# Two passes of eight output rows in a long convolution's inverse transform, and a new order of the work

## The chip, the cores and the metric

The kernel runs on one core of a Trainium2 chip. The core has a matrix engine (TensorE, PE in the profile), a vector engine (VectorE, DVE), a scalar engine (ScalarE, ACT), a slower general engine (GpSimd, POOL), and SyncE (SP), which here only issues DMAs. The engines run their own instruction streams and wait for one another by semaphores. TensorE writes to PSUM, a memory of eight banks, and ACT or DVE must carry each result from there to SBUF (this is called an eviction below). The metric is the device time of one execution in microseconds.

## The reference

`x` is a 2048x448 array in bf16. The kernel computes a gated long convolution with a residual, and then an MLP that mixes along the sequence, with a residual:

```
qn  = layernorm(x)
ks  = sum over t of k_pad[:, t:t+S, :] * shift_k[:, 3-t]     # causal filter of four taps, per channel
kv  = ks * v
y   = irfft( rfft(kv, 2S) * rfft(ssm_k, 2S) )[:S] + kv * ssm_D # long convolution, per channel
h   = x + qn * y
g   = layernorm(layernorm(h))
u   = gelu( einsum("bsd,sf->bdf", g, w1) + b1 )              # 448 x 1792
out = h + ( einsum("bdf,fs->bds", u, w2) + b2 ).transpose    # 2048 x 448
```

## The kernel before

The sequence index is split as s = 16 q + r, with q on the 128 partitions and r (16 "rows" of 448 channels) along the free dimension. The transforms are two small matrix products with a shuffle between partitions in the middle.

The stages, by the names that the order lists use:

- `loads`, `kT`: the filter `ssm_k` arrives channel-major in four chunks of channels (128, 128, 128 and 64) and is transposed on TensorE (L1028). `dummy` products (L1015) stand at the start and between the chunks; they compute nothing that is used.
- `kv`: `k` is transposed (L956), and the four-tap filter is made of small TensorE products with diagonal matrices `DG` (built at L941). In each, two tiles of 64 array rows work side by side (L982). DVE multiplies the result by `v` on its way out of PSUM (L997).
- `k1`, `u1`: the first half of the transform, of the filter and of `kv` (L1049), four tiles of 32 columns side by side; evictions L1059; then a shuffle from SBUF to SBUF by DMAs of the POOL and SP queues (L1065) through a ring of four buffers.
- `k2`, `u2`: the second half (L1084), evicted in place (L728, L729, L731, L732) into `TK` and `TU`, 16 planes each.
- `i1`: DVE multiplies each plane of `TU` with one of `TK`, all four real products at once (L1150), into a ring of four buffers. TensorE applies the inverse of the second half (L1167) to a pair of planes at a time, all 16 output rows in one product of 64 array rows and 128 columns. An eviction (L728) puts the result back into `TU`, and DMAs (L1190, and L1179 for the last pair) shuffle it to `TZ`: for each plane 112 partitions by the POOL queue and 16 by SP.
- `i2`: for each output row r, two products (L1289) read all of `TZ[:, r]`. For rows 0 and 1 the last pair of planes isn't shuffled, and four further products (L1297) with the matrices `EW` take it from where it lies. Each row is then gated, multiplied, normalised by DVE, ACT and POOL (L1306, L1316, L1326, L1332, L1344, L1368), and written as `Q[:, r]` (L1375).
- `q`, `xn`: statistics of the rows of x (L1226, L1228, L1234, L1237), and the first four rows normalised (L1259). `ct` transposes the tables for `i2` (L1098). `warm` is two more dummy products (L1200).
- `mlp`: 7 column blocks of `W1A`, row by row as the rows of `Q` come (L1422), 7 of `W1B` (L1432), gelu (L1412), the second product (L1444) and the output (L1447). The weights come by DMAs of the SP queue: `W1A` (L1395, four quarters), `W1B` (L1399), `W2` (L1406).

The order on every engine is written ahead of time by a planner in the program. Each operation has a due number from `WHEN` (by stage and step, low first), and the planner always starts the ready operation with the lowest number on a free engine, with estimated durations. `WHERE` says for each eviction that could go to either engine whether it is ACT ("a"), DVE ("d") or the planner's choice ("f"). Each engine then runs its instructions, DMA issues included, in that fixed order.

Of the kernel before, what the change touches and what calls it, by code (L numbers as in the profile page):

```python
# [12 lines left out]
    "dummy": (54,),  # L13
    "tables": (137, 107, 179, 164, 70, 80, 73, 176,),
    "loads": (106, 111, 114, 115, 217, 195, 86, 237, 90, 235, 158, 197, 227, 143, 150,),
    "kv": (219, 110, 132, 216, 134, 214, 55, 208, 233, 84, 103, 104, 75, 127, 138, 154, 196,),
    "kT": (60, 57, 218, 64, 231, 198, 146, 78,),
    "k1": (109, 112, 145, 186, 105, 136, 139, 157, 61, 89, 100, 135, 92, 207, 161, 159,),
    "k2": (85, 88, 67, 87, 129, 141, 98, 155, 206, 203, 173, 175, 102, 113, 185, 247,),
    "u1": (68, 81, 99, 116, 131, 147, 144, 169, 172, 174, 210, 229, 65, 97, 140, 223,),  # L20
    "xload": (287, 46, 43, 49,),
    "bias": (193, 277,),
    "q": (213, 278, 298, 222, 309, 50, 94, 204, 279,),
    "u2": (72, 83, 209, 220, 156, 192, 82, 63, 96, 151, 149, 133, 53, 56, 291, 221,),
    "ew": (244,),
    "i1": (272, 29, 45, 194, 122, 263, 123, 91, 128, 273, 148, 265, 71, 74, 38, 189, 126,),
    "ct0": (188, 288,),
    "ct": (225, 3, 302,),
    "xn": (5, 17, 93, 39, 125, 261,),
    "w1a": (205, 303, 163, 286,),  # L30
    "warm": (41, 2,),
    "i2": (304, 9, 299, 58, 124, 22, 66, 234, 79, 305, 1, 160, 108, 23, 13, 310, 21, 42, 162, 6, 202, 10, 120, 18,
        69, 295, 19, 184, 27, 20, 142, 101, 306, 292, 34, 32, 255, 11, 165, 51, 289, 153, 224, 200, 301, 52, 187,
        177, 238, 199, 269, 280, 300, 226, 259, 118, 180, 31, 7, 170, 215, 117, 166, 167, 276, 181, 232, 307, 33,
        296, 4, 76, 77, 14, 182, 283, 168, 30, 293, 95, 47, 152, 12, 183, 270, 28, 37, 16, 40, 171, 36, 308, 44, 239,
        130, 15, 62, 119, 212, 228, 274, 24, 258, 25, 59, 35,),
    "w1b": (211,),
    "w2": (249,),
    "mlp": (190, 240, 8, 178, 297, 26, 48, 201, 290, 230, 121, 0, 241, 243, 275, 242, 260, 294, 418, 419, 420, 421,
        422, 423, 424, 425, 426, 427, 428, 429, 430, 431, 432, 433, 434, 435, 436, 437, 438, 439,),  # L40
}
WHERE = {
    "kv": "ddaadfdd",
    "kT": "ddfdfddd",
    "k1": "faffaffadfaa",
    "k2": "addfffdaffdafffd",
    "u1": "fafdffafafddfffa",
    "bias": "f",
    "u2": "aadafafafaaaffaf",
    "i1": "aaaaffafaaafaffa",  # L50
    "ct0": "d",
    "ct": "fda",
    "xn": "ffff",
    "i2": "afffaaffddfd",
# [89 lines left out]
class _Sched:  # L144
# [161 lines left out]
    def schedule(self):  # L306
# [34 lines left out]
        mode = 0  # L341
# [35 lines left out]
        while done < n:  # L377
            progressed = False
            for e in ENGS:
                if free_at[e] <= t + 1e-9 and ready[e]:  # L380
# [34 lines left out]
                    if o.is_dma:  # L415
                        d0 = free_at[e] + (1200.0 if o.rate != 425.0 else 2000.0)
                        s = max(d0, fab)
                        fab = s + o.nbytes / o.rate
                        fin = max(fab, s + o.nbytes / (o.keng * 27.2))
                        fin += 600.0  # L420
                    else:
                        fin = free_at[e] + self.lat[e]
# [150 lines left out]
def _build(nc, A_q, A_k, A_v, A_shift_k, A_ssm_k, A_ssm_D, B_w1, B_b1, B_w2, B_b2, out):  # L573
# [54 lines left out]
    with ctx:  # L628
# [38 lines left out]
        DG = view(o_DG, [4, 4, 64])  # L667
# [9 lines left out]
        EW = view(o_EW, [4 * NZ, 128], f16)  # L677
        o_ML = o_EW + 1024 * NZ
        ML = [view(o_ML + 256 * k, [128], f16) for k in range(3)]
        assert o_ML + 768 <= o_TU  # L680
# [6 lines left out]
        def MR(s):  # L687
            return view(o_WR + s * 4 * DB, [4, D])
# [11 lines left out]
        mring = _Pool(4)  # L700

        def Pb(b, i=0):
            return PS[:, b.slots[i], 0:D]
# [17 lines left out]
        N_WZ, N_WI, N_W0, N_WK, N_WJ = 2, 0, 9, 3, 0  # L721
# [15 lines left out]
        def emit_tables():  # L737
# [49 lines left out]
            for a, b_, c_ in ((0, 112, 14), (112, 128, 2)):  # L787
                op("pool", lambda e, W, a=a, b_=b_, c_=c_: e.iota(gcm[:, a:b_], [[0, 8], [512, c_]], base=512 * 14 * (a > 0),
# [5 lines left out]
            for k, (b0, st_) in enumerate(((2048, -2048), (2048, 2048), (0, 2048))):  # L794
                for a, b_ in (((0, 128),) if k == 0 else ((0, 112), (112, 128))):
# [77 lines left out]
        def emit_loads():  # L873
            Dq = "sp"
            for i, c in enumerate((0, 1, 2, 3)):
                sch.t0 = -20.0 + i
                op(Dq, lambda e, W, c=c: e.dma_start(KN[0:CW[c], c, :], A_ssm_k[128 * c:128 * c + CW[c], :]),
                   w=[(o_KN + 4096 * c, 4096)], dmab=CW[c] * 4096, rate=217.0 if c == 3 else None)
# [53 lines left out]
        def emit_kv():  # L932
# [3 lines left out]
            for i in range(2):  # L936
# [3 lines left out]
               r=[(o_ID, 256)], w=[(o_I2, 128)], n=64, est=95.0)  # L940
            op("dve", lambda e, W: e.tensor_tensor(  # L941
                out=DG.rearrange("p c j d -> p (c j) d"), in0=I2.unsqueeze(1).broadcast_to([128, 16, 64]),
                in1=wsc.unsqueeze(2).broadcast_to([128, 16, 64]), op=ALU.mult),
               r=[(o_I2, 128), (o_wsc, 64)], w=[(o_DG, 2048)], n=1024, est=1700.0)
# [20 lines left out]
            for g in range(4):  # L965
                for cc in range(2):
                    sch.t0 = T_KV + T_DKV * (2 * g + cc)
# [539 lines left out]
```

## Time and profile before

| | |
|---|---|
| three runs | 174.89, 176.08, 176.18 us; median 176.08 |
| profiled execution | its own time is known as its span alone: 173.7 us from the first to the last instruction |
| median less span | 2.4 us |
| busy in the span | PE 161.4, DVE 103.1, ACT 89.7, POOL 58.8 us |
| DMA | 35.15 MB in 15628 packets |
| granted TensorE clock | 1.000 |

Busy time of PE counts a product from its start to its modelled end, so products that overlap are merged, and a PE that is shown busy is not always at its peak rate.

### The profile page before, as it was taken

How to read it: one execution, taken by the hardware profiler on the slowest of the kernel's cores; microseconds unless marked ns; L12 is line 12 of the kernel's file. 1: busy time of each engine (PE TensorE's matmuls, PEld its weight loads, DVE VectorE, ACT ScalarE, POOL GpSimd, SP SyncE). 2: the span in 40 equal slices, each digit the busy share in tenths (PEclk: the TensorE clock that was granted, in tenths of full speed). 3: DMA queues.
4: the chain of work that ended last, by engine and by line, in shares of the span. 5: the costliest groups of instructions: out<-in, count | busy, mean ns of one | idle time of the engine just before them, and what ended most of it. 6: DMA issues, size and time to landing. Idle time of an engine off the chain costs nothing.

```text
span 173.7 us, 3570 instructions
## 1 busy us (share of the span) xinstructions
PE 161.4 (93%) x1419; PEld 92.1 (53%) x1419; DVE 103.1 (59%) x191; ACT 89.7 (52%) x129; POOL 58.8 (34%) x152
## 2 busy tenths in 40 slices
PE   6989999979989999838999999999999999999994
PEld 2766745442333332424345555555567777777783
DVE  7997899868979999979897751000002132231231
ACT  3796757798999999878883455421120000000000
POOL 8345717680912524564989640000000000000000
PEclk9999999999999999999999999999999999999999
DMA  5999865783859668755999999930000111101111
GB/s 163 408 299 380 284 177 213 301 330 117 244 113 389 198 193 258 246 168 166 392 396 402 416 423 421 417 150 0 0 0 4 53 53 53 44 9 57 53 53 53
DMA packets 15628, 35.15 MB, mean 202 GB/s; under 512 B 3740, under 2 KB 9740, under 8 KB 15612
## 3 DMA queue, kind: packets, MB, share of 16 engines
q1 hardware_dynamic: 12468, 28.25, 44.7%
q0 software_dynamic: 2880, 6.49, 11.4%
q8 instruction: 11, 0.18, 0.4%
q10 hardware_dynamic: 264, 0.18, 0.3%
q14 instruction: 5, 0.04, 0.1%
HBM read 22.05 MB, written 1.84 MB: 137 GB/s over the span
## 4 chain that ended last, share of the span: by engine, by line
PE 61%; DVE 11%; DMA 10%; ACT 8%; POOL 5%; issue 2%; SPq 1%; DVEq 0%; ACTq 0%; POOLq 0%
PE ps L1444 24%; PE ps L1432 12%; PE ps L1422 9%; DMA arena<-arena 6%; DVE arena L1150 5%; DMA arena<-in_A_ssm_k_dram 5%; ACT arena L1059 4%; PE ps L1084 3%; ACT arena L728 3%; PE ps L1049 3%; PE ps L982 2%; PE ps L1167 2%; PE ps L1028 2%; DVE arena L1226 2%; ACT arena L729 2%
## 5 line engine op out<-in xcount | busy, mean ns | idle before, releaser
L1447 DVE SCALAR_TENSOR_TENSOR arena<-ps,arena 128x448 bf16<-128x448 f32 (+2 forms) x17 | 11.1, 656 | 55.7 <-PE ps L1444 55.7
L1444 PE MATMUL ps<-arena 128*128 128x448 bf16 (+2 forms) x238 | 42.7, 342 | 0.0
L1444 PEld LDWEIGHTS ps<-arena 128*128 128x128 bf16 x238 | 33.3, 145 | 9.5
L728 ACT CAST arena<-ps 128x896 bf16<-128x896 f32 (+1 forms) x31 | 24.9, 943 | 1.1 <-PE ps L925 0.6
L1422 PE MATMUL ps<-arena 128*128 128x448 bf16 x112 | 23.1, 353 | 0.9 <-DVE arena L1364 0.6
L1059 ACT CAST arena<-ps 128x896 bf16<-128x896 f32 x23 | 19.5, 913 | 6.6 <-PE ps L1049 6.5
L1065 POOL DMA_DIRECT2D arena<-arena x32 | 17.5, 553 | 13.3 <-ACT arena L1059 12.6
L1432 PE MATMUL ps<-arena 128*128 128x448 bf16 x112 | 21.7, 352 | 0.0
L1084 PE MATMUL ps<-arena 128*64 128x448 bf16 x128 | 16.0, 361 | 1.8 <-ACT arena L1059 0.9
L1412 ACT ACTIVATE arena<-ps,arena 128x448 bf16<-128x448 f32 x14 | 8.2, 640 | 17.5 <-PE ps L1432 15.1
L1150 DVE TENSOR_TENSOR arena<-arena 128x1792 bf16<-128x1792 bf16 x16 | 16.6, 1081 | 0.9 <-DMA arena<-arena 0.9
L1422 PEld LDWEIGHTS ps<-arena 128*128 128x128 bf16 x112 | 10.5, 98 | 12.2 <-DVE arena L1375 3.0
L1432 PEld LDWEIGHTS ps<-arena 128*128 128x128 bf16 x112 | 11.0, 98 | 10.2
L1167 PE MATMUL ps<-arena 64*128 64x448 bf16 x128 | 14.3, 351 | 1.8 <-DVE arena L1150 0.8
L1049 PE MATMUL ps<-arena 128*32 128x448 bf16 x256 | 15.1, 355 | 0.6 <-DVE arena L997 0.3
L1190 POOL DMA_DIRECT2D arena<-arena x14 | 8.2, 589 | 16.4 <-ACT arena L728 16.4
L1344 ACT ACTIVATE arena<-arena 128x448 bf16<-128x448 f32 x14 | 8.1, 575 | 7.1 <-DVE arena L1316 6.9
L1084 PEld LDWEIGHTS ps<-arena 128*64 128x64 f16 x128 | 5.4, 108 | 11.4 <-ACT arena L728 3.8
L1167 PEld LDWEIGHTS ps<-arena 64*128 64x128 f16 x128 | 5.0, 94 | 10.9 <-ACT arena L728 5.3
L1289 PE MATMUL ps<-arena 128*128 128x448 bf16 x32 | 7.7, 353 | 2.6 <-DMA arena<-arena 2.6
L731 DVE COPY arena<-ps 128x1024 bf16<-128x1024 bf16 (+2 forms) x15 | 9.2, 648 | 0.6 <-PE ps L1028 0.6
L1049 PEld LDWEIGHTS ps<-arena 128*32 128x32 f16 x256 | 5.0, 95 | 8.4 <-DVE arena L997 2.6
(96 smaller groups left out, 190.3 us busy)
## 6 DMA issues: line engine op xcount, KB each, us to landing
arena<-in_B_w_dram SPq DMA_DIRECT2D x8, 896.0 KB, 10.3
arena<-in_B_w_dram SPq DMA_DIRECT2D x2, 2048.0 KB, 17.5
arena<-arena SPq DMA_DIRECT2D x16, 224.0 KB, 3.4
arena<-arena POOLq DMA_DIRECT2D x32, 112.0 KB, 3.4
arena<-in_B_w_dram SPq DMA_DIRECT2D x2, 1536.0 KB, 18.9
arena<-arena POOLq DMA_DIRECT2D x14, 196.0 KB, 4.2
arena<-in_A_k_dram SPq DMA_DIRECT2D x4, 448.0 KB, 6.0
arena<-in_A_v_dram SPq DMA_DIRECT2D x4, 448.0 KB, 9.2
```

What stands on the lines that cost most here:

```text
L728: return e.copy(out=dst(), in_=src())
L731: return e.tensor_copy(out=dst(), in_=src())
L1049: op("pe", lambda e, W, b=b, r=r, q=q, x=x, c0=c0: e.matmul(PS[32 * q:32 * q + 32, b.slots[x], 0:D], E[:, 2 * r + x, c0:c0 + 32], src[:, r ...
L1059: return e.copy(out=dst, in_=Ppair(b)) if W == "act" else e.tensor_copy(out=dst, in_=Ppair(b))
L1065: shuf[tag].append(op(q_, lambda e, W, g=g, i=i, a=a, nu=nu, jh=jh: e.dma_start(T[a + i:a + i + 4 * nu - 3:4].rearrange("p (j k) c d -> p ...
L1084: op("pe", lambda e, W, b=bs[h], h=h, j=j, c=c, par=par: e.matmul(PS[64 * par:64 * par + 64, b.slots[c], 0:D], FW[:, 64 * c:64 * c + 64], ...
L1150: op("dve", lambda e, W, m=m, i=i: e.tensor_tensor(out=MR(m.slots[0]).rearrange("p (x y) d -> p x y d", x=2), in0=TU[:, i].unsqueeze(2).br ...
L1167: k = op("pe", lambda e, W, b=bs[h], m=ms[h], par=par, t=t, tab=tab, xy=xy, P=P: e.matmul(Pb(b, par), tab[P, :], MR(m.slots[0])[P, xy, :], ...
L1422: op("pe", lambda e, W, r=r, fc=fc, b=bs[fc]: e.matmul(Pb(b), W1A[:, r, 128 * fc:128 * fc + 128], Q[:, r, :], start=(r == 0), stop=(r == R ...
L1432: op("pe", lambda e, W, r=r, fc=fc, b=b: e.matmul(Pb(b), W1B[:, r, 128 * (fc - n0):128 * (fc - n0) + 128], Q[:, r, :], start=(r == 0), sto ...
L1444: op("pe", lambda e, W, r=r, fc=fc, b=b, d0=d0, d1=d1: e.matmul(Pb(b)[:, d0:d1], W2[fc // 7][:, fc % 7, r:S:R], G[:, fc, d0:d1], start=(fc ...
L1447: op("dve", lambda e, W, r=r, b=b, A=A, d0=d0, d1=d1: e.scalar_tensor_tensor(out=X[:, r, d0:d1], in0=Pb(b)[:, d0:d1], scalar=bm[:, r:r + 1 ...
```

## The change

- **Inverse stage**: all 16 planes of products are kept (four in the old ring's place, the others over planes of `TU` and `TK` that have been read), in the order of pairs `JORD`. `i1` then runs twice over them: pass 0 for output rows 0 to 7, pass 1 (`i1b`) for rows 8 to 15. A product now has 64 array rows and 64 columns, and two pairs of planes are issued together, so that four such tiles stand side by side; in pass 0 the last two pairs go one by one. Each pair is evicted once in each pass, into a staging area in `V`, and shuffled to `TZ` in pieces of 64 partitions, one plane by the POOL queue and one by SP. `W1A`'s first two quarters no longer wait for any shuffle; the other two wait for the last shuffles of pass 0.
- **Filter of four taps**: four tiles of 32 array rows side by side; a unit now covers eight rows of one chunk of 128 channels (or all 16 of the chunk of 64). `DG` is half as large.
- **Last chunk of `ssm_k`**: loaded as 128 half rows, and transposed by pairs of small products into fp32.
- **Less of some things**: dummy products at the start 9 + 1 in place of 9 + 9, `warm` gone, two `EW` products for each of rows 0 and 1 in place of four.
- **New `WHEN` and `WHERE`**; two constants of the planner's DMA model are changed, which act only through the order.

```diff
-    "q": (213, 278, 298, 222, 309, 50, 94, 204, 279,),
-    "i1": (272, 29, 45, 194, 122, 263, 123, 91, 128, 273, 148, 265, 71, 74, 38, 189, 126,),
-    "w1a": (205, 303, 163, 286,),
-    "warm": (41, 2,),
+    "q": (17, 86, 113, 58, 194, 56, 282, 287, 124,),
+    "pr": (140, 148, 178, 259, 39, 47, 190, 98, 153, 77, 76, 167, 65, 68, 129, 265,),
+    "i1": (197, 291, 304, 130, 250, 121, 101, 248, 66, 168, 255, 94, 51, 63,),
+    "i1b": (253, 256, 166, 286, 41, 99, 149, 206, 141, 295, 219, 261,),
+    "xload": (106, 60, 303, 243,),
+    "w1a": (156, 52, 277, 245,),
...
-    "u2": "aadafafafaaaffaf",
-    "i1": "aaaaffafaaafaffa",
+    "u2": "fdaaaaaffaaafafa",
+    "i1": "aaffaaaaa",
+    "i1b": "faffffaa",
...
-                op(Dq, lambda e, W, c=c: e.dma_start(KN[0:CW[c], c, :], A_ssm_k[128 * c:128 * c + CW[c], :]),
+            op(Dq, lambda e, W: e.dma_start(
+                KN[:, 3, 0:S // 2], A_ssm_k[384:448, :].rearrange("c (h s) -> (c h) s", h=2)),
...
+            for u, (g, c) in enumerate(((0, 0), (0, 1), (0, 2), (0, 3), (1, 0), (1, 1), (1, 2))):
+                bs = [_Buf(psum, 2) for _ in range(2)]
+                for m, d in enumerate((0, 4, -3, -2, -1, 1, 2, 3, 5, 6, 7)):
+                    for t in range(4):
+                        i0 = max(0, d)
+                        i1 = min(7, d + 3)
+                        P = slice(32 * t, 32 * t + 32)
+                        b = bs[t // 2]
...
+                            PS[:, b.slots[t % 2], 32 * i0:32 * i1 + 32], KX[c >> 1][P, c & 1, rs, sh:sh + 128],
+                            DG[P, c, i0 - d:i1 - d + 1, :].rearrange("p j d -> p (j d)"),
...
-                if i < 3:
+                if i < 1:
                     dummy(N_WK, T_KT + 1.0 * (2 * i + 1), (k,))
...
+        JORD = (0, 6, 3, 4, 2, 5, 1, 7)
+        def emit_i1(p):
+            groups = [JORD[0:2], JORD[2:4], JORD[4:6]] + ([JORD[6:7], JORD[7:8]] if p == 0 else [JORD[6:8]])
...
+                mt = [x[:, 64 * p:64 * p + 64] for x in (MA, MB, MN)] if not ml else ML
+                for h in range(2):
+                    for t, (tab, xy) in enumerate(((mt[0], 0), (mt[2], 3), (mt[1], 1), (mt[1], 2))):
+                        for par in range(2):
+                            for ip, jj in enumerate(grp):
+                                P = slice(64 * par, 64 * par + 64)
+                                c0 = 64 * (par ^ ip)
...
+                                    PS[c0:c0 + 64, b.slots[h], 0:D], tab[P, :], view(om, [4, D])[P, xy, :],
...
-                       after=shuf["zl"] if h else [shuf["zpool7"]], safter=(wl[0],) if h else ())
+                       after=shuf["zl"] if h > 1 else (), safter=(wl[0],) if h else ())
```

Every quarter of `W1A` has 896 KB; the first two overwrite `KH`, the loaded `k`, which the transposes at L956 read last.

## The prediction

> **What bounds the kernel now.** I read the chain of waits first, to see where the end comes from.
>
> ```profile
> 67.00 2.01 DVE arena L1150 x2
> ...
> 69.81 1.75 ACT arena L728 x2
> 71.56 0.28 issue
> 71.84 0.58 POOL arena L1190
> 72.42 4.51 DMA arena<-arena
> 76.93 0.04 issue
> 76.98 0.55 PE ps L1289 x2
> 77.53 0.77 PE ps L1297 x4
> ...
> 128.71 42.08 PE ps L1444 x231
> ```
>
> The last products of planes, the last evictions, the last shuffle (4.51 us) and then row 0 of the output follow one another. From 90.70 on the chain is TensorE alone to 170.80: the MLP can't be shortened by this change. The timeline shows its first product at 82.66, when the first row of `Q` is ready; between 82.6 and 90.7 TensorE is already 7.77 us busy. So the time is set by when that first row comes, here called S = 82.66, as long as the other rows keep up.
>
> Next, the busy times by stretch, for what limits the way to S.
>
> ```profile
> 20.00:25.00 5.00, 4.69 (x132) 3.44 (x126) 4.76 (x9) 2.36 (x4) 1.95 (x4) 1.00 0.83 254
> 25.00:30.00 5.00, 5.00 (x116) 2.55 (x108) 4.77 (x7) 3.84 (x6) 3.23 (x6) 1.00 0.41 162
> 30.00:35.00 5.00, 4.60 (x92) 1.93 (x84) 4.17 (x7) 3.92 (x6) 2.95 (x6) 1.00 0.78 296
> 35.00:40.00 5.00, 4.35 (x56) 2.07 (x56) 3.65 (x4) 4.56 (x6) 3.52 (x7) 1.00 0.92 348
> 50.00:55.00 5.00, 4.43 (x40) 1.44 (x36) 4.62 (x5) 5.00 (x8) 0.00 (x0) 1.00 0.77 254
> 65.00:70.00 5.00, 4.63 (x40) 1.42 (x38) 5.00 (x7) 4.76 (x7) 2.33 (x4) 1.00 0.86 263
> 75.00:80.00 5.00, 3.02 (x16) 1.58 (x17) 3.78 (x14) 4.54 (x7) 2.13 (x6) 1.00 0.36 102
> ```
>
> The columns are the stretch, then PE, weight load, DVE, ACT and POOL busy, the clock, the DMA share and GB/s. From 20 to 40 PE and DVE are nearly full; from 50 to 70 DVE and ACT are. The groups of the two engines between 50.3 (first plane product) and 72.4 name the work:
>
> ```profile
> L1150 DVE TENSOR_TENSOR arena<-arena 128x1792 bf16<-128x1792 bf16 x16 | 16.6, 1081 | 0.9 <-DMA arena<-arena 0.9
> L1226 DVE BATCH_NORM_STATS2 arena<-arena 128x6 f32<-128x448 bf16 x8 | 4.6, 607 | 0.0
> ...
> L728 ACT CAST arena<-ps 128x896 bf16<-128x896 f32 x29 | 23.9, 971 | 0.5 <-PE ps L1167 0.2
> ```
>
> An eviction of 896 columns follows the last after some 0.92 us on ACT and takes 1.08 us on DVE. Six of the eight statistics rows shown come before the last plane product; with its aggregate (L1228, 0.165) a row costs 0.77 us.
>
> **The change, step by step.** Minus is faster.
>
> Start of the filter. The last chunk's load took 8.5 us to land, the other three 6.1 (table of DMA issues), and TensorE waited 0.37 us for it; its 16 transposes took 1.18 us. 32 products of 64 columns, two tiles at a time, at the 25 to 28 ns that such a step takes in L982, are 0.45 us; two evictions from fp32 cost DVE perhaps 0.2 us each more (414 ns is the nearest 256-column row). Of the eight dummies removed, six (0.73 us each three) fill time in which TensorE waits for the filter until 10.76 anyway; the other three, one kept less, stand in the chain for 0.38 + 0.29 us. But the first product of `k1` at 14.00 also follows a DVE eviction that ends there. Together I take -0.6, between 0 and -1.2.
>
> Filter of four taps. The starts recorded in the trace show two tiles 3 to 4 ns apart and the next pair after 25 ns for 64 columns, 53 for 128, 107 for 256: tiles run side by side and columns set the pace. Before, 208 products took about 6.5 us (3.28 us for 104). After, seven units stream 1024 columns per tile, 427 ns, and the two steps of 32 columns can't be expected below 25 ns: 0.45 us each, 3.2 us in all, 3.3 less on PE. DVE saves half of L941's 1.22 us, 0.6, and 14 multiplications of 684 ns are 9.6 us for 9.5. What of this comes through? From 20 to 40 DVE has 2.65 us idle, and the evictions that the freed PE would feed need ACT or DVE. I take -1.2 for the first plane product (50.3 now), between 0 and -3.3.
>
> The Trainium skill's page "TensorE: Matmul & The Clock Gate", Part 1, says that start-to-start never falls below about 25 ns however small a product is. By that, 308 products would take 7.7 us and the term would be a loss; the 3 ns starts of this trace disagree for products on different tiles.
>
> First pass. Pass 0 evicts 8 pairs in place of 16: 8 x 0.92 = 7.4 us less on ACT and DVE before its last shuffle. Against that stands the order: before, the statistics pairs numbered 50, 94 and 204 ran ahead of the last plane products (189, 126) as six rows; now pairs with 56, 58, 86, 113, 124 and 194 stand ahead of the last products' 259 and 265, so up to twelve rows, 6 x 0.77 = 4.6 us more. Shared between two full engines: (-7.4 + 4.6) / 2 = -1.4. Without the rows it would be -3.7; if all falls on DVE it is a loss (second rival). TensorE's part stays: 128 products at about 95 ns in pairs become 256 at half that; two tiles side by side (L1167, L1084) and four (L1049, starts 4 ns apart, 47 ns each) are the rows on either side of a 64x64 tile. The undoubled last two pairs add 1.5 us, which TensorE has from 55 to 70, where its real work (u2 and i1, some 200 products of 95 ns) is well below the time.
>
> Last shuffle. The chain's 4.51 us is a POOL piece of 196 KB; such pieces land after 4.2 us (median), POOL pieces of 112 KB, the new size, after 3.4. I take -0.8, between 0 and -1.2.
>
> Row 0. Two products of L1297 less, 0.19 us each: -0.4.
>
> Pass 1. Its 8 evictions (7.4 us of two engines) and 6 us of products replace what ran during the wait for the shuffle, which was statistics, `xn` and `ct`. From 72.4 to 77 TensorE is almost idle (2.63 us on the wait alone). Cost at nothing; if the cover is gone, rows 8 to 15 come late. They are needed 8 rows x 9 products x 0.19 = 13.7 us after S, so some 8 us of slip are covered. Their shuffles share SP with two quarters of `W1A` (0.9 MB each, 2.3 us at 400 GB/s): 4.6 us, within that.
>
> `W1A`'s first half. It may go as soon as `k` has been transposed, about 20 us, in SP's queue ahead of its part of the shuffles of `k1` and `u1`. 1.8 MB at 400 GB/s is 4.6 us. The stretch 25 to 30 has 0.59 x 5 = 3 us of DMA time free, so I cost it at 0, with 4.6 as the other end. `warm` (two products at 72.9, where TensorE waits) and the moved `ct` cost nothing.
>
> Sum: -0.6 - 1.2 - 1.4 - 0.8 - 0.4 = -4.4. From the span: 173.7 - 4.4 = 169.3, plus the 2.4 us by which the median of the runs is above it: **171.7 us**. All terms at their low ends would be -9.8, 166.3 us; all at their upper ends -0.4, no change.
>
> **Rivals.**
>
> *Shuffles behind weights* (chance 0.14). For: the chain of waits has a shuffle of 5.07 us at 29.36, after which ACT evicts into the buffer that came free; the DMA share is 0.83 at 20 to 25 and 0.92 at 35 to 40. Against: the hole at 25 to 30. Full price 4.6 us: 171.7 + 4.6 = 176.3, no change.
>
> *Statistics ahead of the last plane products* (chance 0.20), the slow side. Place: DVE between the first product and the last of pass 0. Twelve rows of 0.77 are 9.2 us, the products 16 x 1.04 = 16.6, and one to three evictions of 1.08: about 28 us, against 22.1 now (50.3 to 72.4). In place of -1.4 the term is +5.9, and the time 171.7 + 7.3 = 179.0. It decides once more than seven rows run there: ACT needs 24 x 0.92 = 22 us for its part, which leaves DVE 22 - 16.6 = 5.4 us. For: the numbers in the order, and x landing 4.5 us after its issue at 50.3. Against: the last pair's `u2` eviction has number 288, so DVE may wait for ACT there anyway.
>
> *The four quadrants don't run at once* (0.05). The two row tiles of a pair now write the same bank, where L1167 wrote two. At 95 ns each, 256 products take 24 us; pass 0 ends as before, and pass 1's 12 us meet some 5 us of idle PE: -1.4 is lost and 7 come on top, 171.7 + 8.4 = 180.1. The Trainium skill's page "TensorEngine Tiling (Array Packing)", Restrictions and Gotchas, says that different row tiles can't access one bank at the same time; no row here has two row tiles in one bank, so the trace can't say whether different partitions suffice.
>
> *A step for every small product* (0.03): 308 starts of 25 ns, the pace of the 64-column pairs, are 7.7 us for 6.5: +1.2 for -1.2, 174.1.
>
> *A cold TensorE* (0.05). The first nine dummies are 373 ns apart and later ones 189, although the clock row says full: without dummies between the chunks this could recur. One stretch like the first (3.45 us) costs 1.7: 173.4. Against: the waits there are 0.4 to 1.1 us, and the removed dummies leave at most 2.
>
> **How the numbers follow.** A measurement of this kernel can tell about 1% (1.8 us) from no change. The forecast has 0.53. With the two small rivals, faster by over 1% (below 174.3) has 0.53 + 0.03 + 0.05, less a little for the first of these at the line, 0.59. Within 1%: the weights' rival and that little, 0.16. Slower: 0.20 + 0.05 = 0.25. The range for 8 in 10 reaches from 167.5 to 179.5: it leaves out the quadrants (0.05), the upper part of the statistics rival (0.05) and the forecast's tails. The forecast's own range is 167.5 (short of all low ends at once) to 174.3.
>
> **What would show it.** First plane product before 49.2; the L982 group's successor at about 3.2 us; last eviction of pass 0 some 20.7 us after the first plane product; last shuffle of pass 0 at 3.7 us; first row of `Q` near 78.3, and TensorE without holes from there. Wrong if more than seven statistics rows stand before the last plane product with DVE full, if a shuffle before 50 us takes far over 5 us, if quadrant products start 95 ns apart, or if products of rows 8 to 15 wait for a shuffle.

## The result, and the profile after

| | before | after |
|---|---|---|
| median of four runs each | 176.13 us | 187.53 us (186.72 to 190.38) |
| ratio | | 1.0676, 95% interval 1.0570 to 1.0782 |
| span of the profiled execution | 173.7 us | 185.0 us (its time 186.77) |
| first plane product on VectorE | 50.34 | 54.16 |
| last plane product | 70.45 | 76.22 |
| first product of row 0 | 76.98 | 83.48 |
| first MLP product | 82.66 | 93.38 |
| end of the MLP's products | 170.80 | 182.05 |

The ratios here and below are of the fast runs alone; one of the four runs after, 190.38 us, was in a slow state.

The kernel is slower by 11.4 us where 4.4 us less was forecast. The milestones say where: 3.8 us before the first plane product, 1.95 between the first and the last, 0.7 from there to row 0, and 4.2 from row 0 to the first MLP product. The MLP itself takes about as long as before (88.7 us from its first product to the end, 88.1 before).

The busy times by stretch, with the columns as before (stretch, PE, weight load, DVE, ACT, POOL, clock, DMA share, GB/s):

```profile
25.00:30.00 5.00, 3.12 (x88) 1.52 (x83) 2.86 (x5) 2.70 (x4) 2.07 (x4) 1.00 0.68 201
30.00:35.00 5.00, 3.83 (x100) 1.81 (x92) 3.06 (x5) 4.02 (x5) 4.23 (x8) 1.00 0.83 272
35.00:40.00 5.00, 3.31 (x112) 2.10 (x112) 3.03 (x6) 2.34 (x4) 2.24 (x5) 1.00 0.82 273
...
75.00:80.00 5.00, 4.76 (x66) 2.66 (x58) 4.95 (x12) 4.08 (x6) 1.94 (x4) 1.00 0.47 139
85.00:90.00 5.00, 2.60 (x13) 1.09 (x12) 5.00 (x18) 4.06 (x9) 3.93 (x9) 1.00 0.76 217
90.00:95.00 5.00, 2.30 (x7) 1.00 (x8) 1.97 (x8) 1.34 (x3) 2.52 (x5) 0.78 1.03 386
```

There are two holes. From 25 to 40 none of the three engines is full, although before PE and DVE were; where all are idle in turn, something between them is slow. From 85 to 95 TensorE is half idle, and its granted clock falls (0.78 from 90 to 95). The waits between 18 and 42 us, longest in total first:

```profile
POOL arena L1083 <- ACT arena L1077: 11.2, 7, 3.3
ACT arena L1077 <- PE ps L1067: 8.1, 8, 2.4
DVE arena L1009 <- PE ps L1067: 6.0, 5, 1.8
PEld ps L1067 <- DVE arena L1009: 5.8, 7, 1.4
PE ps L1067 <- DVE arena L1009: 2.8, 4, 1.0
...
DVE arena L1009 <- PE ps L995: 1.7, 2, 0.9
```

The columns are who waits for whom, us in total, times, longest. L1009 is the filter's multiplication on DVE, L995 its products, L1067 the first transform, L1077 its evictions and L1083 its shuffle. DVE and PE wait for each other. DVE's first wait is put down to L1067, with which the filter has nothing to do: the release came late, when PE was already running the next stage. The timeline of one unit shows by how much. First PE, then DVE:

```profile
23.51 1.07 PE L995 MATMUL ps<-arena 32*128 32x128 bf16 x44
24.51 0.95 PE L1067 MATMUL ps<-arena 128*32 128x448 bf16 x16
```

```profile
25.45 1.29 DVE L1009 TENSOR_TENSOR arena<-ps,arena 128x512 bf16<-128x512 f32 x2 [1.18 <-PE ps L1067]
```

The unit's 44 products end at 24.58, and DVE starts on them at 25.45, 0.87 us later; the gap is 0.87 us in all seven units. In the kernel before it was 0.18 us in one unit (32.26 to 32.44) and 0.27 in another (39.13 to 39.40). The trace also records when TensorE's semaphore was raised. Every product raises it once, and from 24.07 to 25.47 us the raises of this unit are 34 or 35 ns apart without a break, while most of its products started 3 to 6 ns apart in fours. So the 44 raises of a unit take 44 x 34.2 = 1.5 us, and the multiplication starts at the last of them. The gap is the same in all units because the backlog stops growing: the raise of the last product comes 0.88 us after its end in each of the seven, and before that the products themselves start 34 ns apart (the last seven of the first unit, 19.00 to 19.21). That is room for some 26 raises, an estimate from 0.88 / 0.0342. The same 34 ns steps are in the trace of before, but there 208 products need 7.1 us of raises and took 6.5 us themselves; now 308 need 10.5 us.

The Trainium skill's page "TensorE: Matmul & The Clock Gate", Part 3, section "The cost: per-tile semaphore tail", states this mechanism: raises by every tile serialise, with a tail of about 25 + 4.7 per tile + 26.3 ns per raise. For 44 tiles that would be an estimated 1.39 us. The section doesn't say from where its tail counts; in the trace the last raise of a unit comes 1.5 us after the end of its first product (31.00 to 32.51) and 0.88 us after the end of its last. The prediction cited that page for another rule and passed over this one.

The second hole, in the chain of waits:

```profile
77.83 5.36 DMA arena<-arena
83.19 0.29 issue
83.48 0.54 PE ps L1317 x2
...
86.06 0.20 POOL arena L1262
86.26 6.39 DMA arena<-arena
92.66 0.05 issue
92.70 0.89 PE ps L1317 x2
93.59 2.24 PE ps L1449 x6
```

L1317 is `i2`, L1449 the MLP. The products of row 8 stand on PE ahead of the first MLP products and wait for a shuffle of pass 1. POOL issued it only at 86.26, 1.1 us after its eviction had ended (85.18), behind work of its own that waited for DVE, and it took 6.39 us, beside the second half of `W1A` (issued from 86.36) and `W1B` (from 88.04).

### The profile page after: what moved, and what is told of

The parts are those of the page before. It is cut to its first block, busy times and chain, and to the rows that moved or that the text cites. A ratio compares the mean times of both kernels' runs of the same rounds, so it can differ in the third digit from the quotient of the medians.

```text
span 185.0 us, 4015 instructions
## 1 busy us (share of the span) xinstructions
PE 166.6 (90%) x1649; PEld 97.9 (53%) x1649; DVE 100.7 (54%) x186; ACT 93.6 (51%) x134; POOL 60.1 (32%) x152
## 4 chain that ended last, share of the span: by engine, by line
PE 63%; DVE 13%; ACT 12%; DMA 6%; POOL 3%; issue 2%; DVEq 0%; ACTq 0%; POOLq 0%
PE ps L1471 23%; PE ps L1449 12%; PE ps L1459 11%; ACT arena L737 8%; DMA arena<-arena 6%; PE ps L1067 4%; PE ps L1189 4%; ACT arena L1077 4%; PE ps L1102 3%; DVE arena L740 3%; DVE arena L1009 3%; PE ps L1317 2%; PE ps L995 2%; DVE arena L1077 2%; DVE arena L836 1%
## 5 line engine op out<-in xcount | busy, mean ns | idle before, releaser
L1471 PEld LDWEIGHTS ps<-arena 128*128 128x128 bf16 x238 | 33.3, 145 | 9.5
L737 ACT CAST arena<-ps 128x896 bf16<-128x896 f32 (+3 forms) x34 | 27.1, 866 | 3.2 <-PE ps L1189 2.3
L1077 ACT CAST arena<-ps 128x896 bf16<-128x896 f32 x23 | 20.0, 913 | 9.3 <-PE ps L1067 8.1
L1449 PE MATMUL ps<-arena 128*128 128x448 bf16 x112 | 24.3, 365 | 0.0
L1083 POOL DMA_DIRECT2D arena<-arena x32 | 17.6, 553 | 17.6 <-ACT arena L1077 13.0
L1459 PE MATMUL ps<-arena 128*128 128x448 bf16 x112 | 21.8, 352 | 0.0
L1189 PE MATMUL ps<-arena 64*64 64x448 bf16 x256 | 19.2, 351 | 0.9 <-ACT arena L737 0.7
L1067 PE MATMUL ps<-arena 128*32 128x448 bf16 x256 | 15.8, 356 | 3.3 <-DVE arena L1009 2.8
L1449 PEld LDWEIGHTS ps<-arena 128*128 128x128 bf16 x112 | 11.3, 101 | 11.2 <-issue 1.5
L1459 PEld LDWEIGHTS ps<-arena 128*128 128x128 bf16 x112 | 11.0, 98 | 10.2
L1189 PEld LDWEIGHTS ps<-arena 64*64 64x64 f16 x256 | 11.1, 106 | 9.0 <-ACT arena L737 2.6
L1212 POOL DMA_DIRECT2D arena<-arena x15 | 8.9, 592 | 18.2 <-ACT arena L737 18.0
L1317 PE MATMUL ps<-arena 128*128 128x448 bf16 x32 | 8.7, 375 | 6.0 <-DMA arena<-arena 6.0
L1009 DVE TENSOR_TENSOR arena<-ps,arena 128x512 bf16<-128x512 f32 x14 | 9.0, 686 | 7.7 <-PE ps L1067 6.0
L1343 DVE SCALAR_TENSOR_TENSOR arena<-arena 128x448 f32<-128x448 bf16 x12 | 8.1, 681 | 7.3 <-ACT arena L1333 7.3
L1333 ACT ACTIVATE arena<-ps,arena 128x448 f32<-128x448 f32 x10 | 7.1, 715 | 9.3 <-PE ps L1317 9.3
(97 smaller groups left out, 185.0 us busy)
```

What stands on the lines that cost most here:

```text
L737: return e.copy(out=dst(), in_=src())
L1009: return e.tensor_tensor(out=v, in0=w_.rearrange("p t (r d) -> p t r d", d=32), in1=v, op=ALU.mult)
L1067: op("pe", lambda e, W, b=b, r=r, q=q, x=x, c0=c0: e.matmul(PS[32 * q:32 * q + 32, b.slots[x], 0:D], E[:, 2 * r + x, c0:c0 + 32], src[:, r ...
L1077: return e.copy(out=dst, in_=Ppair(b)) if W == "act" else e.tensor_copy(out=dst, in_=Ppair(b))
L1083: shuf[tag].append(op(q_, lambda e, W, g=g, i=i, a=a, nu=nu, jh=jh: e.dma_start(T[a + i:a + i + 4 * nu - 3:4].rearrange("p (j k) c d -> p ...
L1189: k = op("pe", lambda e, W, b=bs[jj], om=om, h=h, t=t, tab=tab, xy=xy, P=P, c0=c0: e.matmul(PS[c0:c0 + 64, b.slots[h], 0:D], tab[P, :], vi ...
```

## The experiments

The kernels below ran in sets, each with the kernel before on the same chip, and the ratio is to the kernel before of the same set. Most have four runs; `no_table_transposes` and `filter_alone` have two, `filter_alone_inc` eight, `inc_before` ten. The four last columns are us in the profiled run, one execution each. The recorded expectations call a raise an increment.

| run | median us | ratio, 95% interval | first plane product | last | row 0 | first MLP |
|---|---|---|---|---|---|---|
| inc_filter | 179.42 | 1.0177 (0.9995 to 1.0359) | 50.02 | 72.08 | 78.34 | 86.44 |
| inc_all | 179.21 | 1.0164 (1.0026 to 1.0301) | 48.93 | 70.92 | 77.18 | 86.56 |
| inc_before | 174.74 | 0.9926 (0.9878 to 0.9975) | 49.60 | 69.71 | 75.59 | 82.95 |
| mlp_first | 183.84 | 1.0439 (1.0324 to 1.0554) | 54.32 | 76.39 | 82.65 | 89.59 |
| inc_mlp_first | 178.82 | 1.0165 (1.0093 to 1.0238) | 49.82 | 71.88 | 78.17 | 84.49 |
| pass0_first | 183.52 | 1.0455 (1.0398 to 1.0512) | 49.70 | 71.76 | 80.50 | 89.38 |
| no_table_transposes | 182.59 | 1.0405 (1.0319 to 1.0491) | 50.46 | 72.52 | 79.23 | 89.31 |
| w1_waits | 183.46 | 1.0440 (1.0345 to 1.0535) | 55.64 | 77.70 | 84.98 | 91.29 |
| stats_late | 178.57 | 1.0165 (1.0086 to 1.0244) | 49.21 | 71.27 | 77.53 | 83.85 |
| stats_late_w1 | 178.35 | 1.0151 (1.0084 to 1.0218) | 49.27 | 71.33 | 77.59 | 84.55 |
| norm_late | 179.03 | 1.0208 (1.0116 to 1.0300) | 49.27 | 71.19 | 77.59 | 84.40 |
| norm_stats_late | 178.73 | 1.0176 (1.0095 to 1.0256) | 50.16 | 71.55 | 78.05 | 84.87 |
| filter_alone | 179.88 | 1.0246 (1.0127 to 1.0364) | 55.59 | 75.98 | 81.07 | 87.02 |
| filter_alone_inc | 176.68 | 1.0065 (1.0013 to 1.0118) | 52.31 | 72.71 | 78.37 | 84.06 |
| rows67_late | 178.97 | 1.0217 (1.0144 to 1.0290) | 50.16 | 72.23 | 78.48 | 85.72 |
| rows67_norm_late | 178.16 | 1.0182 (1.0107 to 1.0258) | 48.99 | 69.86 | 77.50 | 83.81 |

**One raise for each wait.** The edit lets the last product that somebody waits for carry the only raise, which counts on products being finished in the order of the program. It is in the planner's last step, with the tag `kv` for the filter alone, without that condition for all stages. The tag takes in the transposes of `k` as well; in the trace of `inc_filter` 22 of the filter's 308 products and 8 of the 80 transposes still raise. In the changed kernel the raise of such a transpose comes at most 0.08 us after its end, so it is the filter's raises that can matter:

```diff
+        keep = set()
+        for o in self.ops:
+            pe = [p for p in set(o.preds) | set(o.extra) if self.ops[p].eng == "pe"]
+            if pe:
+                keep.add(max(pe, key=pos.get))
...
+            elif W == "pe" and o.tag in ('kv',) and oid not in keep:
+                o.fn(self.eng[W], W)
+                o.ev = _Ev(0, W, self.cnt[W] + 1)
```

> The changed kernel with one edit: in the filter, only the last matrix product that somebody waits for raises TensorE's semaphore, instead of all 44 of a unit. Theory A (the semaphore passes one increment per 34 ns, so that 44 increments take 1.5 us and VectorE gets each unit 0.87 us after its last product): the filter's multiplication starts 0.2 to 0.3 us after the last product of its unit, the first plane product comes at 49.5 to 51.5 us instead of 54.2, and the time is 183 to 185.5 us against 187.5. Theory B (the new order, with the transposes of the inverse tables in front, is what delays the filter): the multiplication still follows by about 0.9 us or, if not, the first plane product stays within 0.7 us of 54.2 and the time within 1 us of 187.5.

> The changed kernel with increments on TensorE only where another engine or TensorE itself waits for that very product, in all stages. Theory A: all other stages start their products 46 ns or more apart, above 34 ns, so nothing more is won than in the filter: 183 to 185.5 us, within 1 us of the run with the filter alone. Theory B: no gain, within 1 us of 187.5.

> The kernel before with increments on TensorE only where somebody waits, in all stages. Theory A: its filter has 208 products, its multiplications already follow 0.18 us behind the last product, so the increments are not what bounds it: 175 to 176.5 us, within 1% of 176.1; at most 1.5 us faster. Rival: increments delay every stage by their backlog, then 172 to 174 us.

The filter alone: 187.53 to 179.42 us, and the first plane product 4.1 us earlier. Theory A holds, and the gain is larger than it said. The timeline of the same unit as above, PE and then DVE, in `inc_filter`:

```profile
23.11 0.95 PE L1004 MATMUL ps<-arena 32*128 32x128 bf16 x44
```

```profile
24.14 1.29 DVE L1018 TENSOR_TENSOR arena<-ps,arena 128x512 bf16<-128x512 f32 x2 [0.42 <-PE ps L1004]
```

DVE starts 0.08 us after the products end, where it was 0.87. The part that was not expected is the second hole: in `inc_filter` row 8's shuffle had landed when PE reached its products at 86.03, and the first MLP product came 6.9 us earlier, not 4.1. But the wait there is not gone. In `inc_filter` the granted clock was 0.77 from 80 to 85 us, the 14 products of `i2` before the MLP took 4.51 us (12 took 2.44 in the changed kernel), and so row 8 was reached late. In `inc_all`, whose first plane product comes another 1.1 us earlier, TensorE waits between 76 and 94 us for shuffles again, 4.0 us of it for row 8:

```profile
PE ps L1326 <- DMA arena<-arena: 4.8, 2, 4.0
```

Taking the raises from the other stages as well brings nothing that can be told from no change (179.21). In the kernel before they cost 1.3 us of 176.1, within what theory A allowed: `inc_before` is faster than both kernels.

**The hole before the MLP.** One run moves rows 8 to 15 (the due numbers in its edit) and all that depends on them back in the order by 3 us, one keeps the order and lets the weights wait. In later runs `shift` stands for these 3 us, and `at` is the planned start, raised where a run asks for it; what depends on a moved operation moves with it:

```diff
+            if (o.tag == "i2" and o.eng == "pe" and o.t0 in (173, 89, 205, 46, 237, 210, 213, 220)) or late & (set(o.preds) | set(o.spreds) | set(o.extra)):
+                late.add(oid)
+        order.sort(key=lambda x: (self.start_t[x] + (3000.0 if x in late else 0.0), x))
```

```diff
+            if o.tag in ("w1a", "w1b") and o.t0 in (277, 245, 96):
+                o.extra = o.extra + [x.id for x in self.ops if x.tag == "i1b" and x.is_dma]
```

> The changed kernel with one edit: rows 8 to 15 of the second inverse stage, and all that follows from them, stand 3 us later in the order, so that the products of the first rows of the MLP stand ahead of row 8's on TensorE. Theory C (TensorE's wait of 3.9 us for the shuffle of rows 8 to 15 costs its whole length because MLP products that are ready queue behind it): about 14 MLP products run in the hole, the time falls by 2.5 to 4 us to 183.5 to 185 us, and the clock stays above 0.9 between 90 and 100 us. Rival (the first MLP rows are bound by VectorE's and GpSimd's work on them): the hole is only split, the last MLP product ends less than 1 us earlier, 186.5 to 187.5 us.

> The changed kernel with one edit: the third and fourth quarter of the first weight half and all of the second half wait until the shuffles of rows 8 to 15 have landed. Theory G (row 8's shuffle took 6.4 us, where the same 112 KB took 3.6 us earlier in the stage, because 5.4 MB of weights were started right behind it): TensorE's wait at row 8 falls from 3.9 us to 0.5 to 1.5 us, the first MLP product comes 2 to 3.5 us earlier, the time is 184 to 185.5 us against 187.5. Rival (the shuffle is slow by itself): the wait stays above 3 us, and the weights, started later, cost up to 1 us more: 187 to 188.5 us.

Both theories hold: 183.84 us (3.7 less) and 183.46 us (4.1 less, half a us more than the range said). The waits for shuffles in front of `i2` between 82 and 96 us, in the changed kernel, in `mlp_first` and in `w1_waits`, in us in total, times, longest:

```profile
PE ps L1317 <- DMA arena<-arena: 6.0, 3, 3.9
```

```profile
PE ps L1323 <- DMA arena<-arena: 1.9, 1, 1.9
```

```profile
PE ps L1319 <- DMA arena<-arena: 2.5, 3, 1.0
```

The clock, 0.78 from 90 to 95 us in the changed kernel, is 1.00 in both runs. So the hole had two conditions, a late shuffle and products queued behind it, and taking away either helps. The weights do more: in `w1_waits` the shuffle of row 8, issued at 87.76, has landed when its products start at 90.60, after at most 2.8 us where it took 6.39. From the first product of row 0 to the end of the MLP's products it takes 94.0 us there, as good as the 93.8 of the kernel before, against 95.9 in `mlp_first` and 98.6 in the changed kernel. (The profiled execution of `w1_waits` lost time in the front instead: its granted clock was 0.75 from 30 to 35 us and 0.72 from 40 to 45, and its first plane product came 1.5 us later than in the changed kernel.)

Do the two gains add?

> Both earlier edits at once: the filter's increments only where somebody waits, and rows 8 to 15 of the second inverse stage 3 us later in the order. Theory D (one hole, two ways of filling it: with the filter mended, row 8 was reached at 86.0 us when its shuffle had landed, and TensorE no longer waited there): the two gains of 8 and 3.7 us do not add; 178 to 179.5 us, at most 1.4 us under the run with the filter alone (179.4). Rival (they add): 175 to 176.5 us.

They don't: 178.82 us, 0.6 less than with the filter alone, as theory D said. But the hole is not filled by that. In the chain of waits of this run row 8's shuffle is still there, and longer:

```profile
81.19 6.96 DMA arena<-arena
88.15 0.05 issue
88.19 0.36 PE ps L1335
```

What is left is 2.7 us above the kernel before by the medians. In the profiled executions row 0 comes 1.2 us later than in the kernel before (78.17, 76.98), and a further 2.5 us lie behind it (96.3 us to the end of the MLP's products, 93.8 before). The mended filter with the waiting weights and the rows left in place, which `w1_waits` suggests, was not run.

**The table transposes in front.**

> The run with the filter mended, without the 24 transposes of the inverse tables for rows 4 to 15 and their three evictions (the tables of these rows are set to zero by GpSimd later, in idle time, so rows 4 to 15 of the inverse stage come out as zero). Theory F (in the front they stand in the way of the kernel's transposes and first transforms): the first product of the first forward stage comes at 13.7 to 14.5 us instead of 16.3, the first plane product at 47.3 to 48.3 instead of 50.0, and the time is 2 to 3 us below the run with the filter alone. Rival (the front waits for loads and tables, and the transposes fill idle time): both within 0.7 us of where they were.

The edit leaves `ct`'s operations out of the order and adds the memset. Theory F fails, and both milestones stay where its rival put them: the first product of `k1` came at 15.75 in place of 16.27, the first plane product at 50.46, no earlier. PE's 24 transposes in the front do not set its pace. The time is 3.2 us longer than in `inc_filter`, for the reason of the hole above: TensorE waits 5.6 us there for shuffles, 4.5 of them for row 8's.

**The end of pass 0.**

```diff
+            if o.tag == "i1b" and self.start_t[oid] > 62000.0:
+                at[oid] = max(at[oid], 69700.0 if o.eng == "pe" else 72500.0)
```

> The run before with one more edit: all products of the first pass's last pair stand on TensorE ahead of the 80 products of the second pass that the planner put among them, and the second pass's evictions behind the first pass's. Theory E (the planner counts 47 ns for a quadrant product that takes 93 when it runs in pairs, so the second pass's products hold up the last pair, its shuffle and row 0): the first product of row 0 comes 1.5 to 3 us earlier, at 75.3 to 76.8 us instead of 78.3, the first MLP product 1 to 3 us earlier than in the run before, the time 175.5 to 177.5 us. Rival (the last pair is bound by its plane products and evictions on VectorE and ScalarE): row 0 within 0.7 us of 78.3, the time within 1 us of the run before.

A miss for theory E and for its rival, and 4.7 us slower than the run before it. The busy times show why:

```profile
70.00:75.00 5.00, 3.08 (x36) 1.68 (x28) 4.95 (x11) 3.34 (x5) 2.31 (x5) 0.90 0.43 119
75.00:80.00 5.00, 5.00 (x50) 2.68 (x48) 1.36 (x6) 1.87 (x3) 2.22 (x4) 0.75 0.32 103
```

The last plane product ends at 72.85, but the products of the last pair of pass 0 waited 1.9 us, until 73.40, and by the trace for an eviction on ACT that ended at 73.35. So they started no earlier for being first. The pass 1 products that stood before them had filled idle time. Moved behind them, 48 of them ran until 80.5, at a granted clock of 0.75 from 75 to 80, and row 0 stood behind them.

**From the first to the last plane product.** This stretch is 20.11 us in the kernel before and 22.06 in the changed one, and 22.06 in `inc_filter` and `inc_mlp_first` too. ACT's groups in it, before and then after:

```profile
L728 ACT CAST arena<-ps 128x896 bf16<-128x896 f32 x25 | 20.4, 979 | 0.2 <-PE ps L1167 0.2
```

```profile
L737 ACT CAST arena<-ps 128x896 bf16<-128x896 f32 x23 | 19.3, 921 | 1.1 <-PE ps L1189 1.0
L738 ACT ACTIVATE arena<-ps 128x896 bf16<-128x896 f32 x2 | 1.7, 914 | 0.0
L1287 ACT ACTIVATE arena<-arena 128x448 f32<-128x448 bf16 x2 | 1.4, 764 | 0.0
```

Both have 25 evictions; the changed kernel has two rows of `xn` besides (L1287). DVE holds ten rows' statistics, where before it held six. Six runs, on the base of `inc_mlp_first`, move these in turn; the three conditions are those of `stats_late`, `norm_late` and `rows67_late`, and the others combine them. `stats_late_w1` and `norm_stats_late` have the waiting weights besides, `rows67_norm_late` one raise per wait in all stages; alone, the first left the stretch at 22.06 us (`w1_waits`) and the second at 21.98 (`inc_all`):

```diff
+            if o.tag == "q" and o.eng == "dve" and o.t0 in (58, 56):
+                at[oid] = max(at[oid], 67700.0)
+            if o.tag == "xn" and o.eng == "act" and o.t0 in (128, 221):
+                at[oid] = max(at[oid], 71450.0)
+            if o.tag == "q" and o.eng == "dve" and o.t0 == 194:
+                at[oid] = max(at[oid], 67650.0)
```

> The run with the filter's increments and the MLP's products mended (178.8 us), with the statistics of rows 4, 5, 8 and 9 moved on VectorE behind the last plane product. Theory H (VectorE is full between the first and the last plane product, and holds 10 rows' statistics there, of 0.61 and 0.16 us, where the kernel before holds 6): the last plane product comes 1.5 to 3 us earlier after the first (22.1 us now, 20.1 in the kernel before), row 0 follows 1 to 2.5 us earlier, the time is 176.5 to 178 us. Rival (ScalarE, which is as full with 26 evictions and two normalised rows, feeds the plane products): VectorE idles instead, the last plane product within 0.7 us of where it was, the time 178.5 to 180 us, as the moved statistics now delay the first MLP rows.

> The run with the statistics moved, with the waiting weights as well. Row 8's products no longer stand first in TensorE's queue there, so a faster shuffle is worth little: within 1 us of the run with the statistics alone; if the weights' start is what the MLP's later rows wait for, up to 1.5 us slower.

> The run with the filter's increments and the MLP's products mended (178.8 us), with the two normalised rows that ScalarE works on among its evictions (0.76 us each) moved behind the last eviction of the first pass. Theory I (ScalarE is full from the first plane product to the last: 24 evictions and two normalised rows, where the kernel before has 24 evictions and no row; VectorE's plane products follow its evictions): the stretch shrinks from 22.06 us to 20.2 to 20.7 us, row 0 comes 1.2 to 1.9 us earlier, the time is 176.8 to 178 us. Rival (VectorE, with 10 rows' statistics still in the stretch, becomes the limit at once): 21.3 to 22.06 us, the time 178.3 to 179.3.

> The run with statistics moved and weights waiting (178.4 us), with the two normalised rows moved as well. Theory I: the stretch from the first to the last plane product is 20.0 to 20.5 us, and the time 176.3 to 177.6 us. Rival (evictions of both passes and of the two transforms alone set the pace): above 21.3 us, the time 178 to 179.

> The run with the filter's increments and the MLP's products mended (178.8 us), with the statistics of rows 6 and 7 alone (two of 0.61 and two of 0.16 us) behind the last plane product. Theory J (they stand between the last three plane products on VectorE, and VectorE waits 2.6 us for row 0 afterwards, where they fit in): the stretch from the first to the last plane product is 20.6 to 21.2 us, row 0 comes 0.8 to 1.4 us earlier, the time is 177.2 to 178.2 us. Rival (a last eviction of ScalarE sets the end of the stretch): 21.7 to 22.06 us, and 178.4 to 179.4.

> The same with the two normalised rows behind the last eviction of the first pass, and increments on TensorE only where somebody waits in all stages. Theory J with both in the way: the stretch is 20.0 to 20.7 us, row 0 1.4 to 2 us earlier than in the run without either, the time 176.3 to 177.6 us. Rival: above 21.3 us, 178 to 179.

The stretch came out as 22.06 without the four rows' statistics, 21.92 without the two rows of `xn`, 21.39 without both, 22.07 without the statistics of rows 6 and 7, and 20.87 without those and `xn`. So theories H, I and J fail, and `stats_late`, `norm_late`, `norm_stats_late` and `rows67_late` came out within the ranges of their rivals; `rows67_norm_late` lies between both. Neither engine is the limit by itself: only the pairs give 0.7 and 1.2 us. That the other engine holds the place where one is relieved is the likely reason, not shown. And even 1.2 us less did not come out in the time: 178.16 us against 178.82, with row 0 at 28.5 us after the first plane product in place of 28.35. What is late next is row 0 itself. VectorE's longest wait between 69 and 85 us in `rows67_norm_late`, and between 70 and 84 in `filter_alone_inc`, whose inverse stage is that of the kernel before:

```profile
DVE arena L1376 <- PE ps L1347: 2.8, 1, 2.8
```

```profile
DVE arena L1328 <- PE ps L1299: 0.7, 1, 0.7
```

In the first, row 0 follows the last plane product after 7.64 us. The shuffle that it waits for left at 71.96 and took 5.25 us, and the second pass's products fill TensorE up to 76.55. In the second it follows after 5.66 us.

**The filter by itself.** The kernel before with the new `DG`, products and multiplications of the filter and a new `WHEN` found for it; once with all raises, once with one per wait:

> The kernel before with the four-row-tile filter alone, in an order of its own (the planner's end is 171.4 us, 169.1 for the kernel before). Theory A: the increments (44 of 34 ns for a unit) stretch the front as in the changed kernel: the multiplication follows its unit's last product by 0.8 to 0.9 us, the first plane product comes at 55 to 58 us (50.3 in the kernel before), 181 to 184.5 us. Rival (the increments only matter together with the changed order): 51.5 to 53 us, 176.5 to 179 us.

> The same, with the filter's increments only where somebody waits. Theory A: the first plane product comes 3.5 to 5 us earlier than without, at 51 to 53 us, and the time is 176.5 to 179 us: no better than the kernel before, since VectorE and ScalarE, whose evictions fill the front, have as much to do as with two row tiles. Rival (the filter was what bounded the front): below 49.5 us and below 175.

With all raises the multiplication followed its unit by 0.87 us in two units (30.80 to 31.67, 36.00 to 36.88), as expected, and by 0.66 us in one at a lower granted clock (25.27 to 25.93; the clock was 0.82 from 25 to 30). The first plane product comes at 55.59, with one per wait at 52.31: 3.3 us, a little below what theory A said (3.5 to 5), and the times 179.88 and 176.68 are 3.2 apart. Part of that can be the clock, which was 0.84 and 0.82 between 20 and 30 us in the profiled execution of the first and 1.00 in that of the second. The time of the first is below its range (181 to 184.5). Even with one raise per wait it is no better than the kernel before: 1.0065 (1.0013 to 1.0118). Its order has not been searched as long, so this bounds the filter's worth in that order only.

These two runs also compare the inverse stages. From the first plane product to the first MLP product the one-pass stage takes 31.4 and 31.8 us there, 32.3 in the kernel before and 33.4 in `inc_before`; the two-pass stage takes 39.2 in the changed kernel, 36.4 in `inc_filter` and 34.6 to 35.6 in the runs with rows 8 to 15 moved or the weights waiting (`pass0_first` apart, 39.7).

## Why the prediction was wrong

The range ended at 179.5 us, 8.0 below the result, and none of the rivals was the cause: the nearest, a step for every small product, put 25 ns on the products' starts and 1.2 us on the sum. Point by point:

- **Filter of four taps (-1.2): the step that failed.** The sentence "tiles run side by side and columns set the pace" holds where only a few products raise the semaphore: in `inc_filter` the first unit's products start within 0.47 us (19.25 to 19.71), where 0.45 was forecast. With a raise for each it is false. The products start in fours 3 to 6 ns apart until the backlog is full and then 34 ns apart (0.65 us from first to last in the first unit, 18.55 to 19.21), and the unit is done when its 44 raises are, 1.5 us. Since its four banks stay taken until DVE has read them, PE waits in turn. So the term was a loss where a gain of 1.2 us was forecast. Price: 8.1 us in this order, with what follows from it; 3.2 us in the order that was found for the kernel before, part of which can be the clock. A first sign was in the trace of before, whose semaphore rises in 34 ns steps; the prediction looked at starts only.
- **Start of the filter (-0.6).** Wrong in size and in sign. The last chunk landed in 6.3 us as hoped (8.5 before), but its 32 small products took about 2 us where 0.45 was forecast. Each has a weight load of 194 to 221 ns; that this is what slows them was not tried. The first product of `k1` came 1.6 us later, at 15.58. No effect on the first plane product shows: with one raise per wait it is at 50, with the table transposes or without. That the evictions' work fills the front is likely, not shown.
- **First pass (-1.4).** Measured +1.95 to the last plane product, +1.6 to the start of the shuffle in the chain (23.67 us after the first plane product, 22.08 before). "Pass 0 evicts 8 pairs in place of 16" is right, but the order puts other evictions in their place: from the first to the last plane product there are 25 of them on ACT both before and after, and two rows of `xn`. The statistics rival counted the rows rightly (ten, more than its limit of seven), but its price of 5.9 us is not there: moved away alone, they gave nothing.
- **Last shuffle (-0.8).** The piece in the chain took 5.36 us (+0.85), and 3.49 in `inc_filter` (-1.0). Why it was slow in the changed kernel was not tried.
- **Row 0 (-0.4).** Right: 0.39 us of `EW` products (L1324) where it was 0.77.
- **Pass 1 "at nothing", with 8 us of slip covered: the second step that failed.** The cover was there by need but not by order. Rows 8 to 15 are needed 13.7 us after the first MLP product, but their products stand ahead of that product on TensorE, so the slip begins at zero. And the shuffle is slow beside the weights, 6.39 us against 2.8 at most in `w1_waits`, where the prediction counted the weights as 4.6 us within the slip. That costs 3.7 to 4.1 us. The prediction's last sentence named it among the signs ("if products of rows 8 to 15 wait for a shuffle") and gave it no price.
- **`W1A`'s first half (0).** Its two issues stand in SP's queue before the first shuffle (18.58, 16.43 before). Not tried alone.
- **`warm` and `ct` (nothing).** Right as far as tried: without the transposes the first plane product is not earlier.
- **Quadrants.** Between: the 256 products keep PE busy for 19.2 us, 75 ns each, where 47 and 95 were the two cases. Two products of different row tiles into one bank, in different quadrants, started within 20 ns of each other in 130 of 222 cases. By the rule of the Trainium skill's page "TensorEngine Tiling (Array Packing)", Restrictions and Gotchas, they could not have written that bank at the same time; the trace doesn't agree. The planner's order explains at least part of the rest. It does not issue two pairs of planes together: the 16 products of one stand ahead of the 16 of the other. The first eviction starts at 60.68, right behind the raise of the 16th product (60.65), and up to there the raises come two by two every 0.19 us. So two quadrants, not four, had work side by side for much of the time.

Mending the raises and moving rows 8 to 15 takes away 8.7 of the 11.4 us (`inc_mlp_first`, medians of different sets). The remaining 2.7 belong to the two-pass stage in this order, by comparison with the two runs of the filter alone and not by a run with that stage alone: part is the longer stretch to the last plane product, and the larger part in the profiled executions lies behind row 0, where row 8's shuffle still stands in the chain. Which of the two a better order would give back stays open.

## What to carry to other kernels

Count the semaphore raises of an engine as a resource of their own: with one raise per small product, a group was complete here only n x 34 ns after it began, so raise once for each wait. When a transfer is said to be covered, check where in the engine's fixed order the instruction stands that waits for it: slack counts from that place, not from the need. And where two engines are full in a stretch, relieving one of them, or counting one of them, need not change its length.

## What the runs showed of the hardware that had not been expected

- TensorE's semaphore takes one raise in 34.2 ns, steadily over whole units, however close the products start. When the backlog had grown to 0.88 us, the products themselves started 34 ns apart. The kernel before, with a raise only where somebody waits, is 0.7% faster (0.9926, 0.9878 to 0.9975) without any other edit.
- After a wait of 3.9 us TensorE ran at a granted clock of 0.78 from 90 to 95 us and 0.88 from 95 to 100, and its MLP products started 373 ns apart for a while; in `pass0_first` a wait of 1.9 us before 73.4 us was followed by 0.75 from 75 to 80, in `inc_filter` one of 2.1 us by 0.77 from 80 to 85. Waits as long in `mlp_first` (1.9 us) and `rows67_late` (2.2 us) were followed by 1.00.
- The piece of 112 KB that row 8 waits for took 6.4 us with weights started right behind it and at most 2.8 us with the weights held back until it had landed (`w1_waits`); the median of POOL's pieces in the changed kernel is 3.6.
